# Channel attention with a squared-ReLU FFN: priority for the copies that empty banks, the low parts computed on VectorE, scores over 30 quads, a later first load of weights and tokens

## The chip, the cores and the metric

One NeuronCore of a Trainium2 chip runs the whole program. Its engines work from queues of their own, each in order: TensorE (PE, with its weight loads PEld), VectorE (DVE), ScalarE (ACT), GpSimd (POOL) and SyncE (SP), which here issues all DMAs. The metric is the device time of one execution in microseconds (us), the median of several runs.

## The reference

```python
qn = q / (np.linalg.norm(q, axis=1, keepdims=True) + 1e-06)      # q, k, v: 4 x 6080 x 256
kn = k / (np.linalg.norm(k, axis=1, keepdims=True) + 1e-06)
s = kn.transpose(0, 2, 1) @ qn / tau                             # 256 x 256 for each batch
a = softmax(s, axis=-1)
x = (v @ a).reshape(24320, 256)
h = x @ w_in                                                     # 256 x 2048
out = np.maximum(h, 0.0) ** 2 @ w_out                            # 2048 x 256
```

The norms run along the tokens, so attention is between channels. For each batch there is one small matrix `a`, and `a @ w_in` can be formed once and applied to all tokens of v.

## The kernel before, in words

**Scores.** The host gives k and q side by side as `kq`, 48 tiles of 128 tokens by 512 channels for each batch; `score_load` fetches four tiles (1 MB) into a buffer `kqt` (tag of 3 buffers; for the first loads also the 2 buffers of `g2`). `score_norm` squares two tiles on ACT (L159, `sq`) and adds them to `acc` on DVE (L160). For batches 2 and 3 (the count begins at 0) `score_split` (L162) makes a high part on ACT (L165) and a low part on POOL (L166), both in one `hl` tile of 3 buffers, and `score_burst` multiplies a pair of tiles (12 matmuls of 256 columns, L179) and adds the result on DVE (L184). Batch 0 is scored ahead of everything from unsplit tiles, and the first 32 tiles of batch 1 right behind it (`early_mm`, bank `o`).

**From scores to weights.** `norms` sums `acc` with four tiny matmuls (L208), takes roots and reciprocals in a chain of short DVE instructions (L217 to L223) and builds `diag` (L226); `spread` multiplies it with ones (L233), `exps` makes the softmax, `attnT` transposes (L259). `decode_w_in` turns 64-bit weights into fp32 (L93 to L100), `fold_split` splits them, `fold` multiplies the attention with a quarter of `w_in` (L301, one of the four NG groups), and `combine` makes the seven Strassen operands (`wt`, kept in HBM as `wsc`).

**The main loop.** Tokens come in 6 chunks for each batch, hidden channels in 8 steps: 192 `quads`, 48 for each batch. A quad has seven Strassen products of 3 matmuls (`m1` to `m7`, L384) and the 24 second-layer matmuls of the quad before (`layer2`, L472), in the order of the table `plan` (L608). Product m1 fills a bank `h`; ACT copies it to bank `x` (L416), and only then may m6 add to the same `h` bank; ACT copies that to bank `z` (L423), for m5 and m3. m7 goes to an SBUF tile (L434), which DVE adds twice into `s` (L438). The results are squared and split: `block` with ACT (L392, L393) and DVE (L394, L395) for two of the four, `blocks` with DVE (L404), ACT (L405) and DVE (L406) for the other two.

**What sets the order.** Side work is entered in a table `side` at times counted in quads (`at`, L541 to L595): the pairs of score tiles of batches 2 and 3 are spread from quad 2 to quad 26 of the 48, those of the norms of batch 1 from quad 10 to 26; folding follows, one group in each four quads from quad 30. From the order in which the program is written the framework's scheduler makes one fixed queue for each engine, by priorities and its own estimate of times; what is written under `tc.high_priority()` goes first among the ready.

**The start.** `load_next` takes loads from the list `ring` (L480): five groups of keys, then `load_w_in(0)`, and `load_v(0)` two places later; `decode_w_in(0)` and `fold_split(0, 0)` are written four groups before the last of batch 0 (L507).

Of the kernel before, what the change touches and what calls it, by code (L numbers as in the profile page):

```python
# [10 lines left out]
AF = mybir.ActivationFunctionType  # L11
# [7 lines left out]
def tile_channel_attention_relu2_ffn(ctx, tc, kq, vT, tau, w_in, w_out, outT):  # L19
# [15 lines left out]
    nc = tc.nc  # L35
    B, _, NT, C2 = kq.shape
# [5 lines left out]
    NJ = DFF // P // 2  # L42
# [5 lines left out]
    NGK = NT // G  # L48
# [28 lines left out]
    def h_bank():  # L77
        return ps_h.tile([P, HMAX], F32, name="h", tag="h")
# [42 lines left out]
    def decode_w_in(g):  # L121
        tag = "sq" if g else "vt"
        W = work.tile([P, NH, 2, GW], F32, name=tag, tag=tag, bufs=2 if g else VB)
        decode_f64(raws.pop(("in", g)), W.rearrange("p h t f -> p (h t) f"))
        nc.sync.dma_start(out=wins[g], in_=W)
        win[0, g] = W
# [23 lines left out]
    def score_norm(b, kt):  # L150

        g, t = divmod(kt, G)
        x = kqt[b, g][:, t:t + 2]
        if kt == 0:
            accs[b] = small.tile([P, 2, C2], F32, name="acc")
            nc.scalar.activation(out=accs[b], in_=x, func=AF.Square)
        else:
            sq = work.tile([P, 2, C2], F32, name="sq", tag="sq")
            nc.scalar.activation(out=sq, in_=x, func=AF.Square)  # L159
            nc.vector.tensor_add(out=accs[b], in0=accs[b], in1=sq)  # L160

    def score_split(b, kt):  # L162
        x = kqt[b, kt // G][:, kt % G, :]
        hl = work.tile([P, 2, C2], F32R, name="hl", tag="hl", bufs=HB)
        nc.scalar.copy(out=hl[:, 0], in_=x)  # L165
        nc.gpsimd.tensor_sub(out=hl[:, 1], in0=x, in1=hl[:, 0])  # L166
        split[b, kt] = hl

    def score_mm(b, kt, s, first, last):
# [109 lines left out]
    def fold_split(b, g):  # L279
        W = win.pop((b, g))  # L280
        wi[b, g] = []
        for d in range(NH):
            w = work.tile([P, 2, 2 * GW], F32R, name="hl", tag="hl", bufs=HB)
            x = W[:, d].rearrange("p t f -> p (t f)")
            (nc.vector.tensor_copy if b else nc.scalar.copy)(out=w[:, 0], in_=x)
            nc.vector.tensor_sub(out=w[:, 1], in0=x, in1=w[:, 0])
            wi[b, g].append(w)
# [88 lines left out]
    state = {}  # L376
    gs = {}

    def product(q, i, out, start):
        ci, j = q  # L380
        T = chunks[ci][2]
        w, v = wt[ci, j], vt[ci, i]
        for n, (l, r) in enumerate(((0, 0), (0, 1), (1, 0))):
            nc.tensor.matmul(out=out[:, :T], lhsT=w[:, l, i], rhs=v[:, r, :T], start=start and n == 0,  # L384
                             stop=n == 2, skip_group_check=True)

    def block(q, c, ps, eng):

        T = chunks[q[0]][2]
        r = work.tile([P, HMAX], F32, name="r")  # L390
        hl = work.tile([P, 2, HMAX], F32R, name="g1", bufs=3)
        nc.scalar.activation(out=r[:, :T], in_=ps[:, :T], func=AF.Relu)  # L392
        nc.scalar.activation(out=r[:, :T], in_=r[:, :T], func=AF.Square)  # L393
        eng(out=hl[:, 0, :T], in_=r[:, :T])  # L394
        nc.vector.tensor_sub(out=hl[:, 1, :T], in0=r[:, :T], in1=hl[:, 0, :T])  # L395
        gs[q, c] = hl[:, 0], hl[:, 1]
# [13 lines left out]
    def m1(q):  # L410
        T = chunks[q[0]][2]
        st = state[q] = {}
        st["B"] = h_bank()
        product(q, A11, st["B"], True)
        st["X"] = ps_x.tile([P, HMAX], F32, name="x")
        nc.scalar.copy(out=st["X"][:, :T], in_=st["B"][:, :T])  # L416

    def m6(q):
        T = chunks[q[0]][2]
        st = state[q]  # L420
        product(q, S2, st["B"], False)
        st["Z"] = ps_z.tile([P, HMAX], F32, name="z")
        nc.scalar.copy(out=st["Z"][:, :T], in_=st["B"][:, :T])  # L423

    def m2(q):
        product(q, A12, state[q]["X"], False)
# [2 lines left out]
    def m7(q):  # L429
        T = chunks[q[0]][2]  # L430
        H = h_bank()
        product(q, S3, H, True)
        state[q]["m7"] = work.tile([P, HMAX], F32, name="m7")
        nc.scalar.copy(out=state[q]["m7"][:, :T], in_=H[:, :T])  # L434

    def plus_m7(q, i, ps):
        T = chunks[q[0]][2]
        nc.vector.tensor_add(out=state[q]["s"][:, i, :T], in0=ps[:, :T], in1=state[q]["m7"][:, :T])  # L438

    def m4(q):  # L440
        product(q, A22, state[q]["B"], False)
# [37 lines left out]

    ring = [(score_load, b, g, "g2" if g % 5 > 2 else "kqt") for b in range(2) for g in range(NGK if b == 0 else EARLY)]  # L480
    ring.insert(NGK + 4, (load_w_out, 0))
    ring.insert(8, (load_v, 0))
    ring.insert(5, (load_w_in, 0))
    ring = iter(ring)

    def load_next():
# [9 lines left out]
    for g in range(NGK):  # L496
        for t in range(0, G, 2):
            score_norm(0, g * G + t)
        if g == NGK - 1:
            with tc.high_priority():  # L500
                norms(0)
        for t in range(G):
            kt = g * G + t
            score_mm(0, kt, s0, kt == 0, kt == NT - 1)
        if g == 2:
            load_tau()
        if g == NGK - 4:  # L507
            decode_w_in(0)
            fold_split(0, 0)
        load_next()  # L510
    early = list(range(EARLY * G))
    s1 = ps_o.tile([P, HMAX], F32, name="o11")
# [1 line left out]
    def early_mm(n):  # L514
        for kt in early[:n]:
            score_mm(1, kt, s1, kt == 0, kt == EARLY * G - 1)
            if kt % G == G - 1:
                load_next()
        del early[:n]

    early_mm(2)
    with tc.high_priority():
        spread(0)
        exps(0, s0)
        attnT(0)
        fold(0, 0, 0, ps_z.tile([P, HMAX], F32, name="z"))
        fold(0, 0, 1)
        combine(0, 0)
# [16 lines left out]
    for g in range(1, NG):  # L545
        u = 2 * (g - 1)
# [9 lines left out]
    for i in range(EARLY, NGK):  # L556
        u = i - EARLY
# [2 lines left out]
    QB = NCH * NJ  # L560
    for b in range(1, B):
        u0 = (b - 1) * QB
        first, last = (NJ + 2 if b == 1 else 2), 26
        for i in range(NT // 2):
            u, k = u0 + first + i * (last - first) // (NT // 2), 2 * i
            if k % G == 0:
                at(u - 2.4, score_load, b, k // G)
            at(u - 0.8, score_norm, b, k)
            if b > 1:
                at(u - 1.0, score_split, b, k)  # L570
                at(u - 0.5, score_split, b, k + 1)
                at(u + MID, score_burst, b, [k, k + 1])
        end = u0 + last
        at(end + MID, norms, b)
        at(end + 1 + MID, spread, b)
        at(end + 1.6, lambda b=b: exps(b, s_acc[b]))
        at(end + 2 + MID, attnT, b)
        for g in range(NG):
            u = end + 4 + 4 * g
            at(u - 1.5, load_win, b, g)  # L580
            at(u - 0.5, fold_split, b, g)
            at(u + MID, fold, b, g, 0)
            at(u + 1 + MID, fold, b, g, 1)
            at(u + 1.7, combine, b, g)
# [25 lines left out]
    for n in range(len(quads) + 1):  # L610
        q = quads[n] if n < len(quads) else None
# [37 lines left out]
```

## Time and profile before

| | |
|---|---|
| median of 3 runs | 2206.61 us (2206.30 to 2207.22) |
| the profiled execution | 2210.53 us, span 2208.7 us |
| PE busy | 2174.5 us, 98% of the span, 9848 matmuls |
| PEld busy | 1800.0 us, 81% |
| DVE busy | 1525.9 us, 69% |
| ACT busy | 1398.7 us, 63% |
| POOL busy | 129.8 us, 6%, 96 of its instructions are L166 |
| DMA | 41.8% of 16 engines, 149 GB/s |

A matmul's end is modelled in the profile, and a matmul begins before the one ahead is shown as ended; so the time that PE loses in a wait is more than the idle time shown.

### The profile page before, as it was taken

How to read it: one execution, taken by the hardware profiler on the slowest of the kernel's cores; microseconds unless marked ns; L12 is line 12 of the kernel's file. 1: busy time of each engine (PE TensorE's matmuls, PEld its weight loads, DVE VectorE, ACT ScalarE, POOL GpSimd, SP SyncE). 2: the span in 40 equal slices, each digit the busy share in tenths (PEclk: the TensorE clock that was granted, in tenths of full speed). 3: DMA queues.
4: the chain of work that ended last, by engine and by line, in shares of the span. 5: the costliest groups of instructions: out<-in, count | busy, mean ns of one | idle time of the engine just before them, and what ended most of it. 6: DMA issues, size and time to landing. Idle time of an engine off the chain costs nothing.

```text
span 2208.7 us, 25790 instructions
## 1 busy us (share of the span) xinstructions
PE 2174.5 (98%) x9848; PEld 1800.0 (81%) x9848; DVE 1525.9 (69%) x2124; ACT 1398.7 (63%) x2335; POOL 129.8 (6%) x103
## 2 busy tenths in 40 slices
PE   9999999999999999999999999999999999999999
PEld 7778888888887878888888787888888888888887
DVE  7789866677667676767766768576676665665664
ACT  5578756566766666656676666666665555556564
POOL 0000000000002122100000212110000000000000
PEclk9999999999999999999999999999999999999999
DMA  9748433245444443324544434332453332333331
GB/s 353 291 174 318 158 105 128 104 158 215 162 140 139 145 143 112 110 103 157 212 168 140 146 138 143 112 122 95 169 191 120 134 122 100 122 122 111 110 115 56
DMA packets 68859, 329.35 MB, mean 149 GB/s; under 512 B 7424, under 2 KB 11520, under 8 KB 61184
## 3 DMA queue, kind: packets, MB, share of 16 engines
q1 hardware_dynamic: 68736, 327.71, 41.8%
q8 instruction: 77, 1.26, 0.2%
q14 instruction: 46, 0.38, 0.1%
HBM read 271.32 MB, written 56.36 MB: 148 GB/s over the span
## 4 chain that ended last, share of the span: by engine, by line
PE 73%; issue 14%; DMA 5%; ACT 5%; POOL 3%; DVE 1%; SPq 0%; POOLq 0%; ACTq 0%; DVEq 0%
PE o L472 35%; PE h L384 18%; PE z L384 9%; PE x L384 5%; DMA kqt<-kq 4%; POOL hl L166 3%; PE h L301 2%; PE x L179 2%; PE h L179 2%; PE o L179 1%; ACT sq L159 1%; ACT g L394 1%; ACT hl L165 0%; ACT x L416 0%; ACT r L392 0%
## 5 line engine op out<-in xcount | busy, mean ns | idle before, releaser
L472 PE MATMUL o<-g,woh 128*128 128x512 f32 (+1 forms) x3072 | 1062.4, 388 | 5.6 <-ACT g L405 3.4
L472 PEld LDWEIGHTS o<-g,woh 128*128 128x128 f32 x3072 | 576.3, 188 | 125.5 <-ACT g L405 6.2
L384 PE MATMUL h<-vt,wt 128*128 128x512 f32 (+1 forms) x2304 | 622.5, 392 | 13.3 <-ACT x L416 11.8
L472 PE MATMUL o<-g,wol 128*128 128x512 f32 (+1 forms) x1536 | 595.7, 388 | 0.0
L384 PEld LDWEIGHTS h<-vt,wt 128*128 128x128 f32 x2304 | 427.0, 188 | 121.7 <-ACT x L416 35.3
L405 ACT CAST g<-s 128x1024 fp32r<-128x1024 f32 (+1 forms) x192 | 199.5, 1039 | 419.5 <-DVE s L404 419.4
L395 DVE TENSOR_TENSOR g<-r,g 128x512 fp32r<-128x512 f32 (+1 forms) x384 | 265.6, 692 | 108.3 <-ACT g L394 103.7
L472 PEld LDWEIGHTS o<-g,wol 128*128 128x128 f32 x1536 | 288.4, 188 | 57.3
L384 PE MATMUL z<-vt,wt 128*128 128x512 f32 (+1 forms) x1152 | 325.2, 390 | 6.2 <-DVE s L438 6.2
L406 DVE TENSOR_TENSOR g<-s,g 128x1024 fp32r<-128x1024 f32 (+1 forms) x192 | 233.1, 1214 | 142.1 <-ACT g L405 141.4
L394 DVE CAST g<-r 128x512 fp32r<-128x512 f32 (+1 forms) x192 | 81.2, 423 | 265.5 <-ACT r L393 265.3
L384 PEld LDWEIGHTS z<-vt,wt 128*128 128x128 f32 x1152 | 212.3, 188 | 47.6 <-DVE s L438 8.6
L404 DVE SCALAR_TENSOR_TENSOR s<-s 128x1024 f32<-128x1024 f32 (+1 forms) x192 | 245.2, 1277 | 4.4
L393 ACT ACTIVATE r<-r 128x512 f32<-128x512 f32 (+1 forms) x384 | 241.1, 628 | 9.5
L166 POOL TENSOR_TENSOR hl<-kqt,hl 128x512 fp32r<-128x512 f32 x96 | 129.0, 1362 | 1331.2 <-ACT hl L165 1322.5
L384 PE MATMUL x<-vt,wt 128*128 128x512 f32 (+1 forms) x576 | 161.7, 389 | 0.0
L423 ACT COPY z<-h 128x512 f32<-128x512 f32 (+1 forms) x192 | 109.6, 571 | 76.5 <-PE h L384 76.0
L392 ACT ACTIVATE r<-z 128x512 f32<-128x512 f32 (+1 forms) x192 | 112.9, 588 | 69.9 <-PE z L384 68.7
L160 DVE TENSOR_TENSOR acc<-acc,sq 128x1024 f32<-128x1024 f32 x92 | 112.5, 1223 | 50.6 <-ACT sq L159 48.6
L438 DVE TENSOR_TENSOR s<-z,m 128x512 f32<-128x512 f32 (+1 forms) x192 | 130.6, 680 | 8.8 <-PE z L384 8.4
L438 DVE TENSOR_TENSOR s<-h,m 128x512 f32<-128x512 f32 (+1 forms) x192 | 130.4, 679 | 0.0
L384 PEld LDWEIGHTS x<-vt,wt 128*128 128x128 f32 x576 | 108.2, 188 | 22.5
(112 smaller groups left out, 1698.8 us busy)
## 6 DMA issues: line engine op xcount, KB each, us to landing
wt<-wsc SPq DMA_DIRECT2D x184, 896.0 KB, 4.6
kqt<-kq SPq DMA_DIRECT2D x53, 1024.0 KB, 5.8
wsc<-wt SPq DMA_DIRECT2D x32, 896.0 KB, 5.2
v<-vT SPq DMA_DIRECT2D x40, 512.0 KB, 4.6
outT<-res SPq DMA_DIRECT2D x80, 256.0 KB, 2.6
g<-kq SPq DMA_DIRECT2D x6, 1024.0 KB, 11.5
kqt<-wins SPq DMA_DIRECT2D x12, 512.0 KB, 5.4
v<-vT SPq DMA_DIRECT2D x8, 480.0 KB, 4.2
```

The lines of the kernel that those rows point to most:

```text
L160: nc.vector.tensor_add(out=accs[b], in0=accs[b], in1=sq)
L166: nc.gpsimd.tensor_sub(out=hl[:, 1], in0=x, in1=hl[:, 0])
L179: nc.tensor.matmul(out=s[:, h * C:(h + 1) * C], lhsT=l, rhs=r, start=first and h == 0 and n == 0, stop=last and n == len(terms) - 1, skip_ ...
L384: nc.tensor.matmul(out=out[:, :T], lhsT=w[:, l, i], rhs=v[:, r, :T], start=start and n == 0, stop=n == 2, skip_group_check=True)
L392: nc.scalar.activation(out=r[:, :T], in_=ps[:, :T], func=AF.Relu)
L393: nc.scalar.activation(out=r[:, :T], in_=r[:, :T], func=AF.Square)
L395: nc.vector.tensor_sub(out=hl[:, 1, :T], in0=r[:, :T], in1=hl[:, 0, :T])
L404: nc.vector.scalar_tensor_tensor(out=s, in0=s, scalar=0.0, op0=ALU.max, in1=s, op1=ALU.mult)
L405: nc.scalar.copy(out=h, in_=s)
L406: nc.vector.tensor_sub(out=l, in0=s, in1=h)
L438: nc.vector.tensor_add(out=state[q]["s"][:, i, :T], in0=ps[:, :T], in1=state[q]["m7"][:, :T])
L472: nc.tensor.matmul(out=o[:, :T], lhsT=l[:, wg, wj, es], rhs=r[:, :T], start=first and k == 0, stop=last and k == 2)
```

## The change

`score_split` subtracts on VectorE instead of GpSimd. The copies that empty a bank (Relu of `block`, x, z and m7) and the two additions that read a bank (`plus_m7`) are written under high priority. The first loads of `w_in` and v move behind the twelve groups of keys of batch 0, and their decoding and splitting behind the first two of the early matmuls. Pairs of score tiles of batches 2 and 3 go from quad 0 to 30, norms of batch 1 from 10 to 30, and each batch's folding begins three quads after the new end, at quad 33 instead of 30. The lines below the change shift: Relu is L393, Square L394, the split of `block` L395 and L396, `blocks` L405 to L407, x L418, z L426, m7 L438, `plus_m7` L443, the second layer L477.

```diff
-        nc.gpsimd.tensor_sub(out=hl[:, 1], in0=x, in1=hl[:, 0])
+        nc.vector.tensor_sub(out=hl[:, 1], in0=x, in1=hl[:, 0])
...
-        nc.scalar.activation(out=r[:, :T], in_=ps[:, :T], func=AF.Relu)
+        with tc.high_priority():
+            nc.scalar.activation(out=r[:, :T], in_=ps[:, :T], func=AF.Relu)
...
-        nc.scalar.copy(out=st["X"][:, :T], in_=st["B"][:, :T])
+        with tc.high_priority():
+            nc.scalar.copy(out=st["X"][:, :T], in_=st["B"][:, :T])
...
-        nc.vector.tensor_add(out=state[q]["s"][:, i, :T], in0=ps[:, :T], in1=state[q]["m7"][:, :T])
+        with tc.high_priority():
+            nc.vector.tensor_add(out=state[q]["s"][:, i, :T], in0=ps[:, :T], in1=state[q]["m7"][:, :T])
...
-    ring.insert(8, (load_v, 0))
-    ring.insert(5, (load_w_in, 0))
+    ring[NGK:NGK] = (load_w_in, 0), (load_v, 0)
...
-        if g == NGK - 4:
-            decode_w_in(0)
-            fold_split(0, 0)
...
     early_mm(2)
+    decode_w_in(0)
+    fold_split(0, 0)
...
-        first, last = (NJ + 2 if b == 1 else 2), 26
+        first, last = (NJ + 2 if b == 1 else 0), 30
...
-            u = end + 4 + 4 * g
+            u = end + 3 + 4 * g
```

The z and m7 copies are wrapped as the x copy is. No matmul is added or taken away: both programs hold 9638 TensorE instructions of the same shapes in their queues, and 96 subtractions of 128x512 go from POOL's queue to DVE's.

**ACT in a quad of the score stage of batch 2.** `sq` are the squares of newly loaded keys, `hl` the high parts of tiles, `g2` and `g1` the splits of squared results, `x`, `m7` and `z` the copies out of banks. Before:

```order
L165 CAST hl_6009<-kqt_5708 128x512
L165 CAST hl_6049<-kqt_5918 128x512
L405 CAST g2_6018<-s_6007 128x1024
L392 ACTIVATE r_6034<-z_5973 128x512
L393 ACTIVATE r_6034<-r_6034 128x512
L159 ACTIVATE sq_6477<-kqt_6327 128x1024
L394 CAST g1_6035<-r_6034 128x512
L416 COPY x_6047<-h_6043 128x512
L434 COPY m7_6056<-h_6052 128x512
L159 ACTIVATE sq_6584<-kqt_6327 128x1024
L423 COPY z_6070<-h_6043 128x512
```

ACT in the same quad, after:

```order
L165 CAST hl_6009<-kqt_5731 128x512
L165 CAST hl_6049<-kqt_5918 128x512
L393 ACTIVATE r_6034<-z_5973 128x512
L406 CAST g2_6018<-s_6007 128x1024
L418 COPY x_6047<-h_6043 128x512
L394 ACTIVATE r_6034<-r_6034 128x512
L438 COPY m7_6056<-h_6052 128x512
L395 CAST g1_6035<-r_6034 128x512
L159 ACTIVATE sq_6559<-kqt_6404 128x1024
L426 COPY z_6070<-h_6043 128x512
L393 ACTIVATE r_6075<-x_6047 128x512
```

The copy to x stood two rows behind the first square of a load; it now stands four rows ahead of it.

**DVE ahead of the same place, in the quad whose results `s_6007` are.** Before:

```order
L394 CAST g1_5979<-r_5978 128x512
L395 TENSOR_TENSOR g1_5979<-r_5978,g1_5979 128x512
L184 TENSOR_TENSOR s_acc_5170<-s_acc_5170,h_5990 128x512
L438 TENSOR_TENSOR s_6007<-z_5973,m7_5956 128x512
L438 TENSOR_TENSOR s_6007<-h_5943,m7_5956 128x512
L404 SCALAR_TENSOR_TENSOR s_6007<-s_6007 128x1024
L406 TENSOR_TENSOR g2_6018<-s_6007,g2_6018 128x1024
```

DVE there, after:

```order
L395 CAST g1_5979<-r_5978 128x512
L396 TENSOR_TENSOR g1_5979<-r_5978,g1_5979 128x512
L166 TENSOR_TENSOR hl_6009<-kqt_5731,hl_6009 128x512
L184 TENSOR_TENSOR s_acc_5009<-s_acc_5009,h_5990 128x512
L443 TENSOR_TENSOR s_6007<-z_5973,m7_5956 128x512
L443 TENSOR_TENSOR s_6007<-h_5943,m7_5956 128x512
L166 TENSOR_TENSOR hl_6049<-kqt_5918,hl_6049 128x512
L405 SCALAR_TENSOR_TENSOR s_6007<-s_6007 128x1024
L407 TENSOR_TENSOR g2_6018<-s_6007,g2_6018 128x1024
```

The two subtractions came in, one of them between the additions out of the banks and the squaring of `s`.

**DVE in the norms of batch 0**, from the roots to `diag`. Before:

```order
L217 TENSOR_SCALAR y2_328<-y_324 128x4
L218 RECIPROCAL z_325<-y2_328 128x4
L219 TENSOR_TENSOR z_325<-z_325,h_319 128x4
L220 TENSOR_TENSOR y2_328<-y2_328,z_325 128x4
L221 TENSOR_SCALAR y2_328<-y2_328 128x4
L222 RECIPROCAL z_325<-y2_328 128x4
L223 TENSOR_SCALAR z_325<-z_325,rtau_87 128x2
L226 TENSOR_SCALAR diag_336<-ident_78,z_325 128x128 x2
```

DVE there, after:

```order
L217 TENSOR_SCALAR y2_309<-y_305 128x4
L98 TENSOR_SCALAR hl_341<-hl_341 128x1024
L218 RECIPROCAL z_306<-y2_309 128x4
L99 ISA hl_342<-hl_341,hl_342 128x2048
L219 TENSOR_TENSOR z_306<-z_306,h_300 128x4
L358 TENSOR_TENSOR tt_426<-v_240,tt_424 128x512
L220 TENSOR_TENSOR y2_309<-y2_309,z_306 128x4
L358 TENSOR_TENSOR tt_431<-v_240 128x512
L221 TENSOR_SCALAR y2_309<-y2_309 128x4
L222 RECIPROCAL z_306<-y2_309 128x4
L223 TENSOR_SCALAR z_306<-z_306,rtau_87 128x2
L226 TENSOR_SCALAR diag_317<-ident_78,z_306 128x128 x2
```

Two steps of the decoding and two differences of v came in between the short instructions of the chain.

**PE around the product with `diag`** (`x` is the bank of batch 0's scores, `o11` that of batch 1's early ones). Before:

```order
L179 MATMUL x_107<-kqt_227 128x256 x8
L208 MATMUL h_319<-ones_83,acc_108 128x1 x4
L179 MATMUL o11_353<-kqt_243 128x256 x5
L233 MATMUL h_358<-diag_336,ones_83 128x256
L179 MATMUL o11_353<-kqt_243 128x256 x3
```

PE there, after:

```order
L179 MATMUL x_107<-kqt_220 128x256 x4
L208 MATMUL h_300<-ones_83,acc_108 128x1 x4
L179 MATMUL x_107<-kqt_220 128x256 x4
L179 MATMUL o11_334<-kqt_243 128x256
L233 MATMUL h_358<-diag_317,ones_83 128x256
```

The sums of the norms moved up by four score matmuls, and between them and L233 there are now four score matmuls and one early one instead of five early ones.

## Rows read from the trace of the kernel before

**Rows 1.** The page: busy time, and TensorE's granted clock in 40 slices.

```profile
PE 2174.5 (98%) x9848; PEld 1800.0 (81%) x9848; DVE 1525.9 (69%) x2124; ACT 1398.7 (63%) x2335; POOL 129.8 (6%) x103
...
PEclk9999999999999999999999999999999999999999
```

**Rows 2.** Timeline of PE, 1222 to 1249 us: start, length, line, count.

```profile
1223.51 0.96 PE L384 MATMUL h<-vt,wt 128*128 128x512 f32 x3 [0.52 <-ACT x L416]
...
1231.00 0.84 PE L384 MATMUL z<-vt,wt 128*128 128x512 f32 x3
...
1232.36 1.52 PE L384 MATMUL h<-vt,wt 128*128 128x512 f32 x6
```

**Rows 3.** What PE waited for, 560 to 860 us: idle time, times, longest.

```profile
PE h L384 <- ACT x L416: 6.4, 9, 2.0
PE z L384 <- DVE s L438: 3.7, 3, 1.3
PE o L472 <- DVE g L406: 1.8, 2, 1.6
```

**Rows 4.** The same view, 1110 to 1410 us.

```profile
PE h L384 <- ACT x L416: 5.3, 10, 0.7
PE z L384 <- DVE s L438: 2.5, 2, 1.3
```

**Rows 5.** The chain of waits, 1200 to 1260 us: start, length, what.

```profile
1215.34 1.30 POOL hl L166
...
1216.66 4.73 DMA kqt<-kq
...
1221.41 1.06 ACT sq L159
1222.47 0.51 ACT g L394
1222.98 0.49 ACT x L416
```

**Rows 6.** Timeline of ACT, 1216 to 1226 us.

```profile
1219.00 1.05 ACT L405 CAST g<-s 128x1024 fp32r<-128x1024 f32 x1 [3.02 <-DVE s L404]
...
1222.88 0.58 ACT L416 COPY x<-h 128x512 f32<-128x512 f32 x1
```

**Rows 7.** Groups of DVE, 650 to 850 us: count, busy us, mean ns.

```profile
L404 DVE SCALAR_TENSOR_TENSOR s<-s 128x1024 f32<-128x1024 f32 x16 | 23.7, 1484 | 0.4
...
L372 DVE TENSOR_TENSOR vt<-v,vt 128x512 fp32r<-128x512 f32 x6 | 6.3, 1051 | 0.2
```

**Rows 8.** Groups of DVE, 900 to 1050 us, between the score stages.

```profile
L404 DVE SCALAR_TENSOR_TENSOR s<-s 128x1024 f32<-128x1024 f32 x14 | 17.5, 1251 | 0.2
...
L286 DVE TENSOR_TENSOR hl<-kqt,hl 128x512 fp32r<-128x512 f32 x6 | 4.2, 692 | 0.1
```

**Rows 9.** Timeline of PE, 0 to 60 us (a score matmul shows as two).

```profile
3.63 5.29 PE L179 MATMUL x<-kqt 128*128 128x256 f32 x16 [3.63 <-DMA kqt<-kq]
...
41.10 7.07 PE L179 MATMUL x<-kqt 128*128 128x256 f32 x32
48.01 0.95 PE L208 MATMUL h<-ones,acc 128*128 128x1 f32 x8
48.81 2.40 PE L179 MATMUL o<-kqt 128*128 128x256 f32 x10
51.27 0.70 PE L233 MATMUL h<-diag,ones 128*128 128x256 f32 x2
```

**Rows 10.** Timeline of DVE, 28 to 130 us.

```profile
49.20 0.17 DVE L217 TENSOR_SCALAR y<-y 128x4 f32<-128x4 f32 x1 [1.43 <-ACT y L213]
...
50.73 0.48 DVE L226 TENSOR_SCALAR diag<-ident,z 128x128 f32<-128x128 f32 x2
...
69.84 0.69 DVE L98 TENSOR_SCALAR hl<-hl 128x1024 int32<-128x1024 int32 x1 [0.75 <-ACT hl L96]
70.57 1.23 DVE L99 CUSTOM_DVE_ANT_0 hl<-hl 128x2048 uint16<-128x2048 uint16 x1
```

**Rows 11.** What PE waited for, 0 to 250 us.

```profile
PE o L472 <- ACT g L405: 3.4, 5, 1.6
```

More of the change, by code (lines that the diff above doesn't have):

```diff
@@ L422, in m6 @@
         st["Z"] = ps_z.tile([P, HMAX], F32, name="z")
-        nc.scalar.copy(out=st["Z"][:, :T], in_=st["B"][:, :T])
+        with tc.high_priority():
+            nc.scalar.copy(out=st["Z"][:, :T], in_=st["B"][:, :T])
     def m2(q):
@@ L433, in m7 @@
         state[q]["m7"] = work.tile([P, HMAX], F32, name="m7")
-        nc.scalar.copy(out=state[q]["m7"][:, :T], in_=H[:, :T])
+        with tc.high_priority():
+            nc.scalar.copy(out=state[q]["m7"][:, :T], in_=H[:, :T])
     def plus_m7(q, i, ps):
         T = chunks[q[0]][2]
-        nc.vector.tensor_add(out=state[q]["s"][:, i, :T], in0=ps[:, :T], in1=state[q]["m7"][:, :T])
+        with tc.high_priority():
+            nc.vector.tensor_add(out=state[q]["s"][:, i, :T], in0=ps[:, :T], in1=state[q]["m7"][:, :T])
     def m4(q):
```

## The prediction

> **What bounds the kernel now.** I read the page first: PE is busy for 2174.5 of 2208.7 us [rows 1], and every other engine has a quarter of its time free or more. The matmuls are the same before and after, so the time can change only by what PE loses between them. The next views are what PE waited for, by stretch, and there two stretches stand out: 560 to 860 us and 1110 to 1410 us, the stages in which the scores of batches 2 and 3 are spread over the quads [rows 3, 4]. The reader is to see in them one wait that comes back: product m6 on bank h waits for ACT's copy to x, 19 times.
>
> The idle time shown is not all that a wait costs. Six matmuls in a row take 1.52 us and three 0.84, so one follows another at 0.227 and is drawn 0.39 long [rows 2]; its modelled end covers 0.16 us of every wait. The three matmuls behind a wait take 0.96 instead of 0.84 [rows 2]. So a wait costs its idle time and 0.28 us. The 26 waits of the two stretches show 11.7 us for x, 6.2 for DVE's additions to s, 1.8 for DVE's split of g2, and cost 11.7 + 19 x 0.28 = 17.0, 6.2 + 5 x 0.28 = 7.6 and 1.8 + 2 x 0.28 = 2.4 us, in all 27.0.
>
> Then the chain of waits says why the x copy is late [rows 5]: POOL's subtraction ends and frees a key buffer; the load takes 4.73 us; ACT has been standing at the square of these keys, takes 1.06 us for it, 0.51 for a cast, and only then the x copy. The copy's data were there long before. It began at 1222.88 [rows 6], and PE lost 0.52 + 0.28 = 0.80 us, so it would have been in time at 1222.08. The cast of g2 ahead of it had ended at 1220.05 [rows 6].
>
> **The x copy goes ahead of the square.** In the new ACT order the copy is four rows ahead of the first square of a load, so a late load holds up only the z copy, which PE needs later. The load also starts no later: the buffer is now freed by a subtraction on DVE of about 0.69 us (the nearest row, a split of the same shapes, 0.692 [rows 8]) instead of POOL's 1.30 [rows 5], and loads come every 2.5 quads instead of every 2. What is late next is the cast of g2, which in the new order stands ahead of the x copy and waits for DVE. It had 1222.08 - 1220.05 = 2.03 us to spare. DVE's queue now has one subtraction, 0.69, ahead of the squaring of s, in quads with two squares of keys also a split that slipped back, 0.69; the squaring itself falls from 1.48 to 1.25 without POOL beside it [rows 7, 8]. That is 0.46 to 1.15 us later, and 0.9 or more of the margin is left. So I take off all 17.0 us, and add 2.5 us for new short waits in the 60 quads of the two stages, bounded by 0 and 8 (8 is 0.13 us a quad).
>
> **No work on POOL.** With POOL at work the squaring of s takes 1.48 instead of 1.25 us and the split of v 1.05 instead of the 0.69 of a like instruction [rows 7, 8]. The waits on DVE (s and g2, 10.0 us) lie mostly where a new chunk's v is split among the rest. DVE's added work, 96 x 0.69 = 66 us, falls into quads that have room: DVE is busy 69% of the span [rows 1]. I take 8 of the 10.0 us off, the bounds are 4 and 10. [...]
>
> **Scores over 30 quads, folding later.** One quad in five is now without a pair. The price is at the turn from one batch to the next: the last group's folding, the splits of v and the first keys of the next batch now meet in quads 45 to 48. No row shows this meeting. The nearest are the waits on DVE, about 1.5 us each (7.6 / 5) [rows 3, 4]; two turns, of which one half may be stopped: 1.5 us, with bounds of 0 and 4.
>
> **The start.** In the new DVE queue four long instructions lie between the short ones of the norm chain: L98 (0.69), L99 (1.23) [rows 10] and two differences of v (0.69 each, by the like split [rows 8]), together 3.3 us. They were done among the score work before, hidden behind PE's stream; now PE stands behind them at L233. The chain begins earlier: four score matmuls, 8 passes of 7.07 / 32 = 0.22, now follow L208, so that L208 starts at 48.01 - 1.7 = 46.3 [rows 9]. L217 came 1.19 us after it and L226 ended 2.01 us after L217's start, at 51.21 [rows 9, 10]; now diag is ready at 46.3 + 1.2 + 2.0 + 3.3 = 52.8, less some 0.2 of overlap in the queue. PE arrives at 46.3 + 0.8 (L208) + 1.7 + 0.4 (one early matmul) = 49.2. It waits 3.4 us; before, its ten passes ended at about 51.0 and it waited 0.3 [rows 9]. That is 3.1, say 3.0 us more, with bounds of 0 (if the four are done otherwise) and 4.8. The upper bound comes from the first 16 passes of the program, which follow idle time and take 5.29 us instead of 3.5 [rows 9]: 1.8 us. [...]
>
> Behind it 16 early matmuls that stood between the results of quad 0 now come before the fold, and no longer cover the first g. In the stretch up to 250 us PE waited for such a cast 3.4 us in five waits, 3.4 + 5 x 0.28 = 4.8 in cost [rows 11]. I take one such wait, 1.0 us; bounds are -3 (the x copies of these quads come earlier too) and 4.
>
> Later loads of w_in and v cost nothing of their own: they are issued once the twelfth group of keys has its buffer, about 31 us, and PE has keys to multiply until 48 [rows 9]. If that cover failed, the wait at L233 would grow by the delay.
>
> **The sum.** -17.0 - 8.0 + 2.5 + 1.5 + 3.0 + 1.0 = -17.0 us. The profiled execution took 2210.5, which gives 2193.5 for one like it; the median of the runs lies 3.9 us lower, at 2206.6, and gives **2189.6 us**.
>
> **The rivals.**
>
> *The start costs nothing and all waits go.* If PE's wait at L233 is covered, the sum is -27.0 + 1.0 = -26.0, 2180.6 us. For it speaks that the short instructions have gaps into which long ones might fit; against it that the queue is in order.
>
> *The keys still rule.* Loads come as early as a buffer is free, and squares are placed by the scheduler's estimate of their landing. If the z copy behind the square is then late instead of the x copy, half of the 17.0 stays: -8.5 - 8.0 + 2.5 + 1.5 + 4.0 = -8.5, 2198.1 us. For it speaks that the load in the chain is 4.73 us long [rows 5]; against it that it now starts earlier and has half a quad more.
>
> *VectorE becomes the bound (slower).* If the squaring of s is later by more than the 0.9 us that I find spare, the cast of g2, the x copy and m6 are late in each of the 48 quads with a pair. With 0.35 us in each, 17 us, nothing is won; that is a delay of 1.25 us beyond what I count, two more subtractions in the wrong place. With 0.8 it is 38 us: 2189.6 + 38 = 2228 us. For it speaks one subtraction between the additions and the squaring in every such quad; against it the room on DVE.
>
> *The change does not do what it says*: other waits take over one for one, 2206.6 us.
>
> **How the numbers follow.** Forecast 0.58, start free 0.17, keys 0.13, VectorE 0.06, no change 0.06. About 0.2% (4.4 us) can be told from no change. Faster: 0.58 + 0.17 + 0.10 of the keys' case, 0.85; within 0.2%: 0.03 of it and 0.06, 0.09; slower 0.06. The range for 8 in 10 takes in the forecast with its bounds and most of the second and third cases: 2179 to 2201 us.
>
> **What would show it.** Right: in the new profile's score stages PE has no wait on the x copy worth a microsecond in sum, DVE's squaring of s is at 1.25 us everywhere, POOL is idle, and PE has one wait of some 3 us on diag near 50 us. Wrong: waits of m6 on ACT in most quads with a pair (VectorE's case), waits on the z copy behind squares that wait for keys (the keys' case), no wait on diag (the second), or new waits in the quiet quads after 1700 us, whose order on ACT and DVE is all but unchanged.

## The result, and the profile after

The changed kernel takes 2182.95 us in the median of four runs (2181.15 to 2184.62), the kernel before 2206.91 beside it (2206.30 to 2207.36): a ratio of 0.9891, with a 95% interval of 0.9874 to 0.9909, or 24 us less. Forecast were 2189.6 us and a range of 2179 to 2201. The profiled execution took 2184.62 us, its span is 2182.9.

The page of the kernel after, busy time and granted clock; the first line answers to [rows 1]:

```profile
PE 2162.2 (99%) x9848; PEld 1806.4 (83%) x9848; DVE 1549.7 (71%) x2220; ACT 1385.4 (63%) x2335; POOL 0.8 (0%) x7
...
PEclk9999999999999999999999999999999999999999
```

The 96 subtractions have left POOL and stand on DVE. What PE waited for, from 0 to 250 us, then from 560 to 860 and from 1110 to 1410 us (idle in all, times, longest), which answer to [rows 11, 3, 4]:

```profile
PE h L233 <- DVE diag L226: 2.3, 1, 2.3
PE h L301 <- ACT hl L285: 1.6, 1, 1.6
PE o L477 <- ACT g L406: 1.1, 3, 0.5
```

```profile
PE h L384 <- ACT x L418: 0.6, 2, 0.4
```

```profile
PE h L384 <- ACT x L418: 2.0, 2, 1.5
```

The 19 waits on the x copy in these two stretches are 4, the waits on s and g2 are gone, and a new wait on diag stands at the start. With 30 quads the score stages run on to 959 and 1497 us; there one more wait on the x copy shows, of 0.4 us. The groups of DVE from 650 to 850 us, which answer to [rows 7]:

```profile
L405 DVE SCALAR_TENSOR_TENSOR s<-s 128x1024 f32<-128x1024 f32 x17 | 20.8, 1221 | 0.1
L166 DVE TENSOR_TENSOR hl<-kqt,hl 128x512 fp32r<-128x512 f32 x27 | 18.3, 688 | 1.1 <-ACT hl L165 1.1
```

**What PE loses, stretch by stretch.** The table adds up all that PE loses against its own pace, in us, shown as a wait or not. A quad runs from its first product on bank x to that of the next quad; its loss is that time less its matmuls at the spacing that the same trace has where nothing holds them (0.227 us for 512 columns [rows 2], 0.216 for a pass of the early score matmuls, 0.213 for 480 columns, 0.12 for a pass of the split scores). The head is all ahead of quad 0. The score stages are quads 50 to 73 and 98 to 121; the turns, from one batch to the next, are quads 44 to 49 and 92 to 97; the rest is 10 to 43, 74 to 91 and 122 to 191. In the kernels with 30 quads scores also stand in quads 48, 49, 74 to 77 and 96, 97, 122 to 125, which the table counts to the turns and to the rest. The matmuls are the same everywhere: span less loss is 2144 us in each trace. The labels are those of the runs below.

| trace | head | quads 0–9 | score stages | turns | rest | all |
|---|---|---|---|---|---|---|
| before | 7.4 | 9.3 | 28.6 | 5.3 | 14.1 | 64.8 |
| after | 11.0 | 10.6 | 5.4 | 2.4 | 9.6 | 38.9 |
| b_prio | 7.3 | 7.9 | 18.3 | 2.8 | 5.4 | 41.5 |
| b_dve | 7.4 | 9.4 | 8.3 | 3.3 | 14.4 | 42.8 |
| b_30 | 7.5 | 9.4 | 21.2 | 7.2 | 17.6 | 62.9 |
| b_start | 11.1 | 11.9 | 29.1 | 3.9 | 15.2 | 71.2 |
| pd | 7.5 | 7.9 | 1.3 | 2.5 | 5.8 | 25.0 |
| pd30 | 8.8 | 7.9 | 4.0 | 2.4 | 6.7 | 29.8 |
| a_noprio | 11.8 | 12.0 | 7.0 | 3.9 | 16.1 | 50.7 |
| a_pool | 11.5 | 10.5 | 15.8 | 3.2 | 7.2 | 48.3 |
| after_2 | 11.5 | 10.5 | 4.0 | 2.4 | 7.0 | 35.4 |
| a_oldring | 7.0 | 8.9 | 3.7 | 2.4 | 5.8 | 27.8 |
| a_olddec | 9.4 | 9.2 | 5.9 | 2.4 | 6.9 | 33.7 |
| xd | 7.8 | 8.2 | 1.5 | 3.5 | 5.9 | 26.9 |

The two traces differ by 25.9 us, as their spans do: 23.2 less in the score stages, 2.9 in the turns and 4.5 in the rest, 3.6 more in the head and 1.3 in the first quads. One execution scatters. The head of pd and that of pd30 are the same program, and lose 7.5 and 8.8 us, since in pd30 PE waited 0.9 us for one load of keys that it had in time in pd. after and after_2 are the same kernel, and lie 3.5 apart.

### The profile page after: what moved, and what is told of

It reads as the page before. It is cut to its first block, busy times and chain, and to the rows that moved or that the text cites. A ratio compares the mean times of both kernels' runs of the same rounds, so it can differ in the third digit from the quotient of the medians.

```text
span 2182.9 us, 25772 instructions
## 1 busy us (share of the span) xinstructions
PE 2162.2 (99%) x9848; PEld 1806.4 (83%) x9848; DVE 1549.7 (71%) x2220; ACT 1385.4 (63%) x2335; POOL 0.8 (0%) x7
## 4 chain that ended last, share of the span: by engine, by line
PE 90%; DMA 4%; ACT 4%; DVE 2%; issue 1%; SPq 0%; ACTq 0%; DVEq 0%
PE o L477 43%; PE h L384 22%; PE z L384 11%; PE x L384 5%; PE h L179 3%; DMA kqt<-kq 2%; PE h L301 2%; PE x L179 2%; DMA v<-vT 1%; PE o L179 1%; ACT g L406 1%; ACT r L393 0%; DVE s L443 0%; DVE s L405 0%; ACT x L418 0%
## 5 line engine op out<-in xcount | busy, mean ns | idle before, releaser
L477 PE MATMUL o<-g,woh 128*128 128x512 f32 (+1 forms) x3072 | 1065.7, 388 | 1.7 <-ACT g L406 1.1
L477 PEld LDWEIGHTS o<-g,woh 128*128 128x128 f32 x3072 | 576.4, 188 | 119.9 <-ACT g L406 2.7
L384 PE MATMUL h<-vt,wt 128*128 128x512 f32 (+1 forms) x2304 | 615.4, 389 | 6.0 <-ACT x L418 4.8
L477 PE MATMUL o<-g,wol 128*128 128x512 f32 (+1 forms) x1536 | 595.7, 388 | 0.0
L384 PEld LDWEIGHTS h<-vt,wt 128*128 128x128 f32 x2304 | 431.4, 188 | 98.5 <-ACT x L418 9.6
L396 DVE TENSOR_TENSOR g<-r,g 128x512 fp32r<-128x512 f32 (+1 forms) x384 | 262.9, 685 | 130.0 <-ACT g L395 124.8
L477 PEld LDWEIGHTS o<-g,wol 128*128 128x128 f32 x1536 | 288.4, 188 | 57.3
L407 DVE TENSOR_TENSOR g<-s,g 128x1024 fp32r<-128x1024 f32 (+1 forms) x192 | 233.1, 1214 | 137.4 <-ACT g L406 136.9
L394 ACT ACTIVATE r<-r 128x512 f32<-128x512 f32 (+1 forms) x384 | 241.4, 629 | 8.0
L395 DVE CAST g<-r 128x512 fp32r<-128x512 f32 (+1 forms) x192 | 81.1, 422 | 227.3 <-ACT r L394 225.3
L405 DVE SCALAR_TENSOR_TENSOR s<-s 128x1024 f32<-128x1024 f32 (+1 forms) x192 | 232.6, 1211 | 2.8
L393 ACT ACTIVATE r<-z 128x512 f32<-128x512 f32 (+1 forms) x192 | 113.2, 589 | 169.8 <-PE z L384 163.6
L426 ACT COPY z<-h 128x512 f32<-128x512 f32 (+1 forms) x192 | 109.9, 572 | 64.7 <-PE h L384 64.0
L443 DVE TENSOR_TENSOR s<-z,m 128x512 f32<-128x512 f32 (+1 forms) x192 | 130.4, 679 | 8.8 <-PE z L384 8.6
L443 DVE TENSOR_TENSOR s<-h,m 128x512 f32<-128x512 f32 (+1 forms) x192 | 129.9, 677 | 0.0
L393 ACT ACTIVATE r<-x 128x512 f32<-128x512 f32 (+1 forms) x192 | 113.8, 593 | 12.2
```

The lines of the kernel that those rows point to most:

```text
L405: nc.vector.scalar_tensor_tensor(out=s, in0=s, scalar=0.0, op0=ALU.max, in1=s, op1=ALU.mult)
L407: nc.vector.tensor_sub(out=l, in0=s, in1=h)
L477: nc.tensor.matmul(out=o[:, :T], lhsT=l[:, wg, wj, es], rhs=r[:, :T], start=first and k == 0, stop=last and k == 2)
```

## The experiments

In the three series of runs below the kernel before took 2211.9, 2212.5 and 2211.5 us, 5 more than beside the changed kernel above and close to its profiled execution, 2210.5. So ratios are compared within a series, and the table's losses between traces.

### Each of the four parts alone

b_prio is the kernel before with priority on five lines, of which this is one:

```diff
-        nc.scalar.copy(out=st["X"][:, :T], in_=st["B"][:, :T])
+        with tc.high_priority():
+            nc.scalar.copy(out=st["X"][:, :T], in_=st["B"][:, :T])
```

> The kernel before with the priority of the five bank-emptying lines alone. Theory (the square of a key load standing ahead of the x copy costs the 17 us of the two score stages, and what moves it behind is the earlier release of key buffers, not the priority): in this kernel's ACT order the square still stands right ahead of the x copy in 17 of the loads, so the waits of m6 on the x copy stay, 8 to 14 us shown at 560 to 860 and 1110 to 1410 us, and the time is 2203 to 2209 us. Rival (the priority is what takes the x copy out of the wait for keys): the waits go, and the time is 2188 to 2193.

b_dve moves the subtraction:

```diff
-        nc.gpsimd.tensor_sub(out=hl[:, 1], in0=x, in1=hl[:, 0])
+        nc.vector.tensor_sub(out=hl[:, 1], in0=x, in1=hl[:, 0])
```

> The kernel before with the subtraction of score_split on DVE instead of POOL alone. Theory: the buffer is free sooner, the square stands behind the x copy in 17 of the loads, the waits on the x copy fall under 2 us in the two stages, the squaring of s falls from 1.48 to about 1.22 us, the waits on s and g2 fall by 8 of 10 us: 2182 to 2189 us. Rival (priority is needed for the x copy): only the 8 to 10 us of s and g2 go, 2197 to 2199. Second rival (DVE, with 66 us more work, gets late): over 2203.

b_30 spreads the scores, with the later folding:

```diff
-        first, last = (NJ + 2 if b == 1 else 2), 26
+        first, last = (NJ + 2 if b == 1 else 0), 30
...
-            u = end + 4 + 4 * g
+            u = end + 3 + 4 * g
```

> The kernel before with the scores of batches 2 and 3 over 30 quads and the folding later, alone. Theory: the square still stands ahead of the x copy in about 10 loads instead of some 14 to 20, POOL still beside DVE, so that a third to a half of the 17 us goes and little of the 10: 2196 to 2203 us. Rival (the spread itself, with more time for each load, is what helps): 2186 to 2192. Second rival (the turns cost what the quads gain): 2205 to 2209.

b_start loads and decodes the first weights later:

```diff
-    ring.insert(8, (load_v, 0))
-    ring.insert(5, (load_w_in, 0))
+    ring[NGK:NGK] = (load_w_in, 0), (load_v, 0)
...
-        if g == NGK - 4:
-            decode_w_in(0)
-            fold_split(0, 0)
...
     early_mm(2)
+    decode_w_in(0)
+    fold_split(0, 0)
```

> The kernel before with the later loads of w_in and v and the later decoding alone. Theory (the decoding in DVE's queue now stands in the norm chain, and the stop of PE behind it costs about 4.2 us with the slower passes that follow, and the first quads another 1): 2209.5 to 2212.5 us. Rival (covered): 2206 to 2207.5.

| alone | median, us | ratio to before | 95% interval |
|---|---|---|---|
| b_prio | 2187.64 | 0.9896 | 0.9879 to 0.9912 |
| b_dve | 2188.80 | 0.9900 | 0.9885 to 0.9914 |
| b_30 | 2208.84 | 0.9990 | 0.9981 to 0.9999 |
| b_start | 2217.64 | 1.0026 | 1.0014 to 1.0038 |

The theory held for the subtraction, by its ratio and with one wait of 0.4 us on the x copy left in the two stages, and nearly for the start, whose 5.8 us are just above the 5.6 that it allowed. For b_prio it fell, though not where it was drawn up. The waits on the x copy did stay, if fewer, as what PE waited for in the two stages of b_prio shows:

```profile
PE h L384 <- ACT x L418: 3.5, 7, 1.6
PE z L384 <- DVE s L443: 0.9, 2, 0.5
```

```profile
PE h L384 <- ACT x L418: 2.5, 7, 0.5
PE z L384 <- DVE s L443: 1.0, 2, 0.5
```

Beside [rows 3, 4] that is 6.0 us for x instead of 11.7 (8 to 14 were expected), 1.9 for s instead of 6.2, none for g2. But the table puts 10.3 of its 23.3 us into the score stages only; 8.7 lie in the rest, where the wait view of before shows next to nothing. One quad of that stretch shows how. PE in the kernel before, then in pd, at the same place of the last chunk (start, length, count):

```profile
1703.58 0.38 PE L472 MATMUL o<-g,woh 128*128 128x480 f32 x1
1703.87 0.92 PE L384 MATMUL h<-vt,wt 128*128 128x480 f32 x3
```

```profile
1666.28 0.38 PE L477 MATMUL o<-g,woh 128*128 128x480 f32 x1
1666.49 0.81 PE L384 MATMUL h<-vt,wt 128*128 128x480 f32 x3
```

Product m6 began 0.29 us behind the matmul ahead instead of 0.21, and its three took 0.92 instead of 0.81: 0.19 us lost, and no idle time shown, since the modelled end of 0.38 covers the gap. In quads 140 to 191 of before, 12 starts on bank h were late like this one, by 0.03 to 0.09 us, in b_prio and pd none. In before two casts, of v and of g, stand on ACT between the square and the x copy of that quad; in pd both come behind the copy.

In the score stages one quad can be followed through three kernels. These are ACT in the kernel before, in b_prio and in b_dve, at the square of the same load (the bracket is idle time and what ended it), and PE's wait behind it in the first two:

```profile
694.07 1.06 ACT L159 ACTIVATE sq<-kqt 128x1024 f32<-128x1024 f32 x1 [1.59 <-DMA kqt<-kq]
695.03 0.60 ACT L371 CAST vt<-tt 128x512 fp32r<-128x512 f32 x1
695.54 0.61 ACT L394 CAST g<-r 128x512 fp32r<-128x512 f32 x1
696.06 0.57 ACT L416 COPY x<-h 128x512 f32<-128x512 f32 x1
...
696.69 0.97 PE L384 MATMUL h<-vt,wt 128*128 128x512 f32 x3 [1.98 <-ACT x L416]
```

```profile
687.31 1.06 ACT L159 ACTIVATE sq<-kqt 128x1024 f32<-128x1024 f32 x1 [1.58 <-DMA kqt<-kq]
688.27 0.58 ACT L418 COPY x<-h 128x512 f32<-128x512 f32 x1
...
688.90 0.96 PE L384 MATMUL h<-vt,wt 128*128 128x512 f32 x3 [1.62 <-ACT x L418]
```

```profile
695.48 1.06 ACT L159 ACTIVATE sq<-kqt 128x1024 f32<-128x1024 f32 x1
```

Priority takes the two casts out from between square and copy; the square itself stays ahead, and ACT still stands 1.58 us at it. With the subtraction on DVE the square is elsewhere in ACT's order and doesn't wait. Of the 36 key loads among the quads, the first square stands at most three rows ahead of an x copy in 20 before, 20 in b_prio, 12 in b_30, 4 in b_dve and 4 in the changed kernel; of the 24 loads of batches 2 and 3 in 18, 16, 10, 2 and none. Why a subtraction on another engine moves squares on ACT isn't in the traces; that the scheduler reckons with an earlier free buffer is only argued.

b_30 missed what was expected, and came nearest to its second rival: its score stages lose 7.4 us less, but the turns 1.9 and the rest 3.5 more. The loss in the turns lies where scores now stand too: quads 49 and 97, with an x copy behind a square of keys, lose 2.3 us more than before. Of the loss in the rest 2.5 us lie in one quad, 144, where ACT's copy of results, ahead of the x copy, stood 1.95 us waiting for a store of earlier results.

### The parts together

pd is priority and subtraction on DVE, with 24 quads and the old start; pd30 has 30 quads as well; a_noprio is the changed kernel without priority, a_pool with the subtraction back on POOL. Their edits are the pieces shown above, put together or taken back; of a_pool, against the changed kernel:

```diff
-        nc.vector.tensor_sub(out=hl[:, 1], in0=x, in1=hl[:, 0])
+        nc.gpsimd.tensor_sub(out=hl[:, 1], in0=x, in1=hl[:, 0])
```

> Priority and the subtraction on DVE together; scores over 24 quads and the start as before. Theory (the two do different things: the subtraction on DVE clears the two score stages, the priority clears the small waits on the x copy in all the other quads; so their gains add up there, and the start of the changed kernel costs 6 us): 33 to 38 us under the kernel before of the same call, ratio 0.983 to 0.985, some 10 us under the changed kernel. Rival (they remove the same waits, each alone already 23 us): 23 to 27 us under before, ratio 0.988 to 0.990.

> The changed kernel with the start as before: priority, subtraction on DVE, 30 quads. Theory (the later loads and decoding cost 6 us): 29 to 32 us under the kernel before, ratio 0.9855 to 0.987; beside the run with 24 quads it is 1 to 4 us slower, since the turns with the later folding cost more than the score quads still win. Rival (30 quads help): faster than the run with 24 quads by 1 us or more.

> The changed kernel without priority: subtraction on DVE, 30 quads, the new start. Theory (priority clears small waits outside the score stages, 8 to 12 us): 4 to 10 us slower than the changed kernel, 14 to 20 us under before, ratio 0.991 to 0.994. Rival (priority does nothing beside the subtraction on DVE): 23 to 25 us under before, ratio 0.989.

> The changed kernel with the subtraction back on POOL: priority, 30 quads, the new start. Theory: the waits on the x copy behind squares come back in part, 4 to 8 us in the two score stages: ratio 0.991 to 0.993, 16 to 20 us under before. Rival (priority and 30 quads clear them without the subtraction's move): 23 to 25 us under before, ratio 0.989.

| | median, us | ratio to before | 95% interval |
|---|---|---|---|
| pd | 2170.84 | 0.9814 | 0.9799 to 0.9829 |
| pd30 | 2174.47 | 0.9831 | 0.9816 to 0.9846 |
| a_noprio | 2197.27 | 0.9934 | 0.9918 to 0.9951 |
| a_pool | 2194.71 | 0.9922 | 0.9907 to 0.9937 |

The two parts add up for the most part, beyond the 33 to 38 us that the theory gave: 24 and 23 us alone, 41.7 together, 5.6 less than their sum, since both take from the score stages and the turns. The subtraction on DVE clears the score stages (28.6 to 8.3), the priority the other quads (14.1 to 5.4), both together leave 1.3 and 5.8. In pd PE has no wait at all of 0.2 us or more from 560 to 860 and from 1110 to 1410 us; the four longest entries of the whole run, all of them outside these stretches, are:

```profile
PE x L179 <- DMA kqt<-kq: 4.3, 2, 3.6
PE o L477 <- ACT g L406: 1.1, 3, 0.5
PE h L384 <- ACT x L418: 0.8, 1, 0.8
PE o L477 <- DVE g L407: 0.6, 1, 0.6
```

On top of these two the 30 quads cost 3.6 us. That is the size expected, but not for its reason, since the turns lose 2.5 us in pd and 2.4 in pd30; the score stages lose 2.7 more. The keys come at other moments of a quad, and at some of their loads ACT stands at a square again. The longest such place in the changed kernel, on ACT and on PE:

```profile
1253.43 2.01 ACT L159 ACTIVATE sq<-kqt 128x1024 f32<-128x1024 f32 x2 [3.85 <-DMA kqt<-kq]
...
1257.23 0.60 ACT L418 COPY x<-h 128x512 f32<-128x512 f32 x1
...
1257.88 0.96 PE L384 MATMUL h<-vt,wt 128*128 128x512 f32 x3 [1.46 <-ACT x L418]
```

a_noprio and a_pool have the ratios that the theory gave. Against the changed kernel the gap is larger than expected for both: beside after_2, which ran in another series, they are 16.4 and 13.9 us slower. a_pool loses 15.8 us in the score stages (b_prio 18.3), a_noprio 16.1 in the rest (b_dve 14.4). What came back in a_pool is only in part what its theory named, the waits on the x copy. From 560 to 860 and from 1110 to 1410 us more of it are waits on DVE's additions to s, as the two longest entries of each stretch show; the squaring of s takes 1404 ns from 650 to 850 us.

```profile
PE z L384 <- DVE s L443: 2.6, 3, 1.2
PE h L384 <- ACT x L418: 1.4, 4, 0.4
```

```profile
PE z L384 <- DVE s L443: 2.4, 4, 1.2
PE h L384 <- ACT x L418: 1.3, 4, 0.4
```

**Which priority.** xd has the subtraction on DVE and, of the five priorities, that of the x copy alone, the diff shown for b_prio.

> The kernel before with the subtraction on DVE and priority for the x copy alone (not for the relu, the z copy, the m7 copy and the additions to s). Theory (outside the score stages the small losses are all of products on bank h, behind the x copy): the same as with all five, 2169 to 2173 us. Rival (the other priorities, the relu's above all, carry part of it): 2176 to 2187.

It took 2172.76 us, ratio 0.9825 (0.9809 to 0.9842), beside 0.9814 for all five in another series. So, with the subtraction on DVE, the one line carries nearly all of it.

### The start

after_2 is the changed kernel again. a_oldring has its late decoding, but the loads of w_in and v where they were; a_olddec its late loads, but the decoding where it was. The edits of the two against the changed kernel, one after the other:

```diff
-    ring[NGK:NGK] = (load_w_in, 0), (load_v, 0)
+    ring.insert(8, (load_v, 0))
+    ring.insert(5, (load_w_in, 0))
```

```diff
+        if g == NGK - 4:
+            decode_w_in(0)
+            fold_split(0, 0)
...
     early_mm(2)
-    decode_w_in(0)
-    fold_split(0, 0)
```

> The changed kernel again, beside the next three, so that they can be compared on one chip. It should lie 8 to 10 us above what the kernel with the start as before and else the same would give here (2174.5 in its own call, so 2182 to 2185 us), with PE's wait at L233 of 2.3 us and at L301 of 1.6 us.

> The changed kernel with the loads of w_in and v where they were (6th and 9th), and the decoding still late in the program. Theory: DVE's order then has nothing long between L217 and L226, the wait on diag falls from 2.3 to under 0.4 us and the slow passes behind it with it; the fold still comes late, so the wait of L301 on hl stays at 1.5 to 3 us: 4 to 6 us under the changed kernel, 2177 to 2180. Rival (what costs is that the decoding is late, wherever the long instructions stand in the chain): less than 2 us under the changed kernel.

> The changed kernel with the late loads, and the decoding where it was written before, at the ninth group of keys. Theory: L98, L99, L100, one difference of v and the two of L286 now stand between L217 and L226, 0.7 + 1.2 + 1.2 + 3 x 0.7 = 5.2 us instead of 3.3; the wait at L233 grows from 2.3 to 3.5 to 4.5 us with slow passes behind it, and the wait of L301 falls from 1.6 to 0.5: within 2 us of the changed kernel, 2181 to 2185. Rival (the place of the decoding decides): as with the start before, 2174 to 2177 us.

| | median, us | ratio to before | 95% interval |
|---|---|---|---|
| after_2 | 2180.86 | 0.9861 | 0.9847 to 0.9876 |
| a_oldring | 2175.78 | 0.9837 | 0.9823 to 0.9852 |
| a_olddec | 2180.23 | 0.9859 | 0.9844 to 0.9874 |

after_2 lies 6.4 us above pd30 instead of 8 to 10, with PE's two waits as expected, 2.3 us at L233 and 1.6 at L301. The old ring takes back 5.1 us, as expected, and leaves about 1 us to pd30; the old place of the decoding takes back 0.6 us, which can't be told from nothing. (By the table it takes back 3.4 us in the head and the first quads and loses 1.9 in the score stages; that second part may be scatter.) So it is the late loads that cost, through the order that they bring to DVE. The wait on diag is gone in a_oldring, where DVE has nothing long between L217 and L226; that at L301 fell further than expected, to 0.9 us. In a_olddec PE's wait grew less than expected, to 2.6 us instead of 3.5 to 4.5, since six more early passes stand ahead of it; that at L301 is 1.3 us instead of 0.5.

The place itself, in the changed kernel, on DVE and on PE, answers to [rows 10, 9]:

```profile
47.16 0.17 DVE L217 TENSOR_SCALAR y<-y 128x4 f32<-128x4 f32 x1 [4.22 <-ACT y L213]
47.24 0.69 DVE L98 TENSOR_SCALAR hl<-hl 128x1024 int32<-128x1024 int32 x1
47.84 0.17 DVE L218 RECIPROCAL z<-y 128x4 f32<-128x4 f32 x1
47.96 1.23 DVE L99 CUSTOM_DVE_ANT_0 hl<-hl 128x2048 uint16<-128x2048 uint16 x1
...
49.17 0.68 DVE L358 TENSOR_TENSOR tt<-v,tt 128x512 f32<-128x512 f32 x1
...
49.84 0.69 DVE L358 TENSOR_TENSOR tt<-v 128x512 f32<-128x512 f32 x1
...
50.99 0.48 DVE L226 TENSOR_SCALAR diag<-ident,z 128x128 f32<-128x128 f32 x2
```

```profile
45.97 0.95 PE L208 MATMUL h<-ones,acc 128*128 128x1 f32 x8
46.78 1.97 PE L179 MATMUL x<-kqt 128*128 128x256 f32 x8
48.59 0.59 PE L179 MATMUL o<-kqt 128*128 128x256 f32 x2
51.53 1.07 PE L233 MATMUL h<-diag,ones 128*128 128x256 f32 x2 [2.34 <-DVE diag L226]
52.39 4.11 PE L179 MATMUL o<-kqt 128*128 128x256 f32 x12
56.34 0.38 PE L259 MATMUL h<-ident,e 128*128 128x128 f32 x2
```

From L208 to L259 it is 10.37 us for the same matmuls that took 6.38 before (48.01 [rows 9] to 54.39): the stop costs 4.0 us. Of these, 1.7 come behind the wait: L233's two take 1.07 instead of 0.70, and the 12 passes 4.11 instead of 2.75 (before, 51.80 to the same count). The granted clock fell, from 1.00 to a mean of 0.62 from 51 to 54 us and of 0.81 from 54 to 57, in a stretch that the page's 40 slices are too coarse to show. Busy time of PE, PEld, DVE, ACT and POOL, granted clock, DMA share and GB/s by window, in the changed kernel and in a_olddec:

```profile
48.00:51.00 3.00, 1.18 (x6) 0.70 (x4) 2.93 (x10) 0.63 (x2) 0.00 (x0) 1.00 0.52 164
51.00:54.00 3.00, 2.47 (x6) 2.01 (x7) 1.43 (x6) 0.37 (x1) 0.00 (x0) 0.62 1.02 429
54.00:57.00 3.00, 3.00 (x14) 2.42 (x14) 0.90 (x4) 1.09 (x4) 0.00 (x0) 0.81 0.98 389
```

```profile
48.00:51.00 3.00, 2.25 (x11) 1.64 (x9) 3.00 (x7) 1.16 (x4) 0.00 (x0) 1.00 0.14 55
51.00:54.00 3.00, 1.17 (x5) 1.06 (x6) 2.40 (x8) 0.75 (x2) 0.00 (x0) 1.00 1.19 330
```

In a_olddec the stop was longer, 2.58 us, and the granted clock stayed at 1.00: there the 12 passes behind it take 2.75 us, as before.

## Why the prediction was right, and where it wasn't

**The sum.** Trace against trace the kernel gained 25.9 us where 17.0 were forecast. The turns came out 4.4 us better than their term and the rest, which had no term, 4.5; the score stages were 0.7 better, the head and the first quads 0.9 worse. So the terms of the score stages and of the start held, and what lifted the gain above the forecast are two places that the prediction had wrong. That the time fell inside the range has some luck in it: in the series of after_2 the same change gained 30.6 us (2211.49 to 2180.86), more than the 27.6 from the forecast's 2206.6 to the lower end of its range.

**The score stages: right in sum, and for a reason that was only half given.** Forecast were -17.0 - 8.0 + 2.5 = -22.5 us, and the table has 28.6 - 5.4 = 23.2. The chain square, casts, x copy [rows 5] is what held PE, and each link can be taken out by itself. But the prediction put the copy's new place down to the change as a whole, and b_prio and b_dve show that the square goes behind the copy with the subtraction on DVE, not with the priority. The keys' case is there in small, though on the x copy and not on the z copy: 0.6 us of x waits in two quads between 560 and 860 us and 2.0 us in two between 1110 and 1410, where no wait worth a microsecond in sum was forecast.

**POOL.** The squaring of s fell from 1484 to 1221 ns [rows 7], as said, and the waits on s and g2 went wholly, 10.0 us by their cost where 8 were taken off: with all of them the sum would have been 2 us nearer. Why the squaring takes longer with POOL at work no trace shows, and that work doesn't carry those waits alone: in b_prio POOL is at work, the squaring takes 1453 ns, and of the 8.0 us of idle time behind DVE 6.1 are gone all the same, by order. In a_pool, with priority too but another spread of the scores, 5.0 us of waits on s are there. How much of b_dve's gain is the shorter instruction and how much the order wasn't separated. DVE's group in b_prio from 650 to 850 us:

```profile
L405 DVE SCALAR_TENSOR_TENSOR s<-s 128x1024 f32<-128x1024 f32 x16 | 23.2, 1453 | 0.3
```

**The turns: the step that set +1.5 failed.** It supposed that folding, splits of v and first keys meet in quads 45 to 48 and stop PE there. They don't: with their like in the second turn, 93 to 96, these quads lose 4.8 us before, 4.3 in b_30, which has the later folding alone, and 1.6 both in pd, without it, and in the changed kernel. In the changed kernel the turns lose 2.9 us less. Priority alone takes 2.5 off there and the subtraction 2.0, and neither was in that term.

**The rest was missed.** For the quads outside the score stages the prediction had no term, since the wait view shows nothing there and the order seemed all but unchanged. They lost 14.1 us. Of these, 6.9 lie in products on bank h, 31 of which start 0.03 to 0.24 us late, mostly under the modelled end; pd and b_prio have no such late start. Most of the other 7.2 stays in pd, whose rest loses 5.8. Priority brings the rest to between 5.4 and 7.2; the changed kernel's profiled execution has 9.6, its second one 7.0. The step that failed is the price of a wait: idle time and 0.28 us is right for a wait that is shown, but waits that are not shown were counted as none.

**The start: right in mechanism, size within its bounds.** The stop is where it was forecast, behind the four long instructions, with PE there at 49.18 us (49.2 forecast). Diag was ready at 51.47 instead of 52.8: L217 to the end of L226 takes 4.31 us, 2.3 more than before [rows 10] and not 3.3. Before, L218 began 0.20 us behind L217, as the line below shows beside [rows 10]; now L98 begins 0.08 behind it, ahead of its shown end, and L218 0.60 behind L98, which is 0.69 long. So the wait was 2.3 us longer than before, and the slow passes, at a granted clock of 0.62 and then 0.81, made it 4.0, against 3.0 in the sum and an upper bound of 4.8, which had them at 1.8. In a_olddec a stop of 2.58 us brought no fall of the clock (1.00 from 48 to 57 us), so the length of the stop alone does not decide it. DVE in the kernel before:

```profile
49.40 0.18 DVE L218 RECIPROCAL z<-y 128x4 f32<-128x4 f32 x1
```

**The first quads.** Forecast was +1.0 for one wait on the cast of g. The 16 early matmuls were indeed a cover that went, and a new wait on DVE's split of g (L396, 0.5 us) is there. But the larger thing that lay under the cover was the second fold: PE stands 1.62 us at L301, instead of 0.5 before, for weights whose decoding (L98, L99, L100) has just ended on DVE. The new start costs 2.6 us in these quads, by b_start against before and by after_2 against pd30; priority takes 1.4 off, so that the table has 1.3 more than before. PE, ACT and DVE there:

```profile
98.24 0.50 PE L301 MATMUL h<-hl,aTh 128*128 128x512 f32 x1 [1.62 <-ACT hl L285]
```

```profile
97.57 0.62 ACT L285 CAST hl<-sq 128x512 fp32r<-128x512 f32 x1 [3.28 <-DVE sq L100]
```

```profile
96.31 1.23 DVE L100 SCALAR_TENSOR_TENSOR sq<-hl 128x1024 uint32<-128x1024 uint32 x1
```

**The rivals.** By its time alone the result stands nearer to 2180.6, "the start costs nothing and all waits go", than to the forecast. The trace decides against that: the start costs some 6 us in all, and what makes up for it lies in the turns and the rest, for which neither case had a gain. VectorE, with 66 us more work, did not become the bound; pd has that work too.

**The better kernel.** Priority and subtraction on DVE without the other two parts take 2170.84 us, 1.9% under the kernel before. The 30 quads and the later loads lose some 10 of it again: 3.6 (pd30 against pd) and 6.4 (after_2, 2180.86, against pd30, in different series).

## What to carry to other kernels

Before costing an edit, add up what the bound engine loses against its own pace, over every stretch and not only where the wait view has rows: here 8.7 of the 23.3 us that priority alone took off lay in the rest, where the wait view shows nothing. A copy that empties a bank for the next matmul should have nothing in front of it in its queue that waits for a transfer (in b_prio ACT stood 1.58 us at such a square, and PE 1.62 at the product behind the copy), and where an order is made by a scheduler, each edit is to be looked up in the order that it makes, since the edit that moved the square was the one on another engine. A load that is put off moves its consumers too, and they may come to stand in a short chain that the bound engine waits for (here diag came 2.3 us later in its chain, and PE stood 2.34 us at L233).

## What the runs showed of the hardware

The granted clock fell behind a stop of 2.34 us (from 1.00 to a mean of 0.62 and then 0.81 in windows of 3 us; PE had done 8 and 2 score passes since the sums of the norms, and the 12 passes behind took 4.11 us), and in b_start, a_noprio, a_pool and after_2 behind a stop of 2.3 us (mean granted clock 0.50 to 0.95 in the windows from 51 to 54 and 54 to 57 us), but not behind 2.58 us in a_olddec, where 8 and 8 passes came first (1.00). Which of the differences decides isn't settled.

DVE's chain of short instructions, each of which needs the one before, took 2.01 us alone, nine instructions from L217 to L226 [rows 10]. With four independent long ones between them, 3.29 us together, it took 4.31, so 1.0 us of the long ones cost nothing: each of the four, and the short one behind it, begins 0.05 to 0.09 us before the one ahead is shown as ended.
